# Decode attention on one core: halving the first half of K twice, and reading it from one PSUM bank

## Chip, cores, metric

One core of a Trainium2 chip. The metric is the device time of one execution in microseconds. "Ratio" below is the mean time of one kernel's runs over the mean of the other's runs of the same rounds, so it is not quite the ratio of the medians that I quote. Each comparison has its own runs of the kernel before, on the same chip.

## The reference

Attention with one query row per head: 8 x 32 = 256 heads, 4096 keys and values of 128 each, all bf16.

```python
B, H, Sq, Skv, Dh = 8, 32, 1, 4096, 128
def reference(q, k, v):
    scale = q.shape[-1] ** -0.5
    scores = jnp.einsum('bhqd,bhkd->bhqk', q, k) * scale
    attn = _softmax(scores, axis=-1)
    return jnp.einsum('bhqk,bhkd->bhqd', attn, v)
```

Every byte of K and V is used once. There is no reuse, so the kernel has to read 537 MB and do very little with each byte.

## The kernel before

A tile is eight heads: 16 partitions per head, 256 key rows on each partition (C = 256), 64 KB per partition. There are NT = 32 tiles of K and 32 of V, and SLOTS = 3 buffers that both share.

A K tile is worked on like this. VectorE multiplies it with the query in place, then adds the upper half of the 128 columns to the lower half (width 64), and for part of the tile once more (width 32). TensorE then adds what is left: it multiplies slices of 8 columns with an identity matrix and accumulates them in one bank of PSUM, the memory that matmuls write to (512 sums per partition and bank). VectorE reduces the bank's last axis to one score per key row.

```python
UC = 64; DS = 512 // UC; NU = C // UC          # 64 rows x 8 sums in a bank, 4 parts of a tile

def width_of(t, u):
    return D // 4 if u >= NU // 2 and 0 < t < NT - 3 else D // 2

def product(t, lo, hi):                        # VectorE
    ...
    nc.vector.tensor_tensor(out=part, in0=part, in1=qb[:].to_broadcast([P, hi - lo, D]), op=ALU.mult)
    nc.vector.tensor_tensor(out=part[:, :, 0 : D // 2], in0=part[:, :, 0 : D // 2],
                            in1=part[:, :, D // 2 : D], op=ALU.add)
    if width_of(t, lo // UC) < D // 2:
        nc.vector.tensor_tensor(out=part[:, :, 0 : D // 4], in0=part[:, :, 0 : D // 4],
                                in1=part[:, :, D // 4 : D // 2], op=ALU.add)

def sum_over_d(t, u):                          # TensorE, then scores_of on VectorE
    ps = ps_s.tile([P, UC, DS], F32, name="ps", tag="ps")
    n = width_of(t, u) // DS
    for s in range(n):
        nc.tensor.matmul(ps[:], lhsT=ident[:],
                         rhs=kt[:, u * UC : (u + 1) * UC, s * DS : (s + 1) * DS],
                         start=(s == 0), stop=(s == n - 1))
```

So in tiles 1 to 28 the first half of the rows goes to TensorE at width 64 (two banks of eight matmuls), the second at width 32 (two banks of four).

The order within a steady tile, shortened:

```python
product(t, 0, 2 * Q); sum_over_d(t, 0); sum_over_d(t, 1)      # Q = C // 4
product(t, 2 * Q, 3 * Q); sum_over_d(t, 2)
scores_of(t, 0); scores_of(t, 1)
product(t, 3 * Q, C); sum_over_d(t, 3); scores_of(t, 2)
values_loop(t - 1)                 # TensorE, 64 matmuls over the V tile before
load("k", t + 1); load("v", t)     # each is issued when a buffer comes free
scores_of(t, 3); weights_of(t)
```

With three buffers, V tile t goes where K tile t was, and is issued when TensorE has summed the last part of K tile t. The K tile after next goes where V tile t - 1 was, and is issued when the loop over it ends.

Of the kernel before, what the change touches and what calls it, by code (L numbers as in the profile page):

```python
# [8 lines left out]
ALU = mybir.AluOpType  # L9
AX = mybir.AxisListType  # L10
BF16 = mybir.dt.bfloat16
F32 = mybir.dt.float32
# [13 lines left out]
def kernel(  # L26
# [7 lines left out]
    nc = tc.nc  # L34
    B, H, Sq, D = q.shape
    S = k.shape[2]
    P = nc.NUM_PARTITIONS
# [3 lines left out]
    C = S // PH  # L41
    NT = NH // G
    scale = float(D) ** -0.5
    UC = 64
    DS = 512 // UC
    NU = C // UC
    CB = 4
    RG = R * G
    NQ = NT // R
# [18 lines left out]
    ps_s = ctx.enter_context(tc.tile_pool(name="ps_s", bufs=3, space=bass.MemoryType.PSUM))  # L68
# [7 lines left out]
    ident = consts.tile([P, P], BF16, name="ident")  # L76
    nc.gpsimd.memset(ident[:], 0.0)
    nc.gpsimd.affine_select(
        out=ident[:], in_=ident[:], pattern=[[-1, P]], compare_op=ALU.not_equal,
# [6 lines left out]
        out=heads[:], in_=heads[:], pattern=[[-1, G], [0, PH]], compare_op=ALU.not_equal,  # L86
# [6 lines left out]
        out=own[:], in_=own[:], pattern=[[-PH, G]], compare_op=ALU.is_ge,  # L93
# [3 lines left out]
        out=own[:], in_=own[:], pattern=[[PH, G]], compare_op=ALU.is_ge,  # L97
# [5 lines left out]
        out=same[:].rearrange("p (h x) -> p h x", x=PH),  # L103
        in_=own[:].rearrange("p (b h) -> p h b", h=TB // PH)
        .rearrange("p h (o b) -> p h o b", o=1)
        .to_broadcast([P, TB // PH, PH, P // TB]),
        axis=AX.X, op=ALU.max,
# [4 lines left out]
    for j in range(TG):  # L112
        part = pick[j * AG : (j + 1) * AG, :, :, :]
        nc.gpsimd.affine_select(
            out=part, in_=part, pattern=[[-1, CB], [CB * G, R], [-CB, RG]],
# [6 lines left out]
        out=mine[:], in_=mine[:], pattern=[[PH * G, R], [-PH, RG]], compare_op=ALU.is_ge,  # L122
# [3 lines left out]
        out=mine[:], in_=mine[:], pattern=[[-PH * G, R], [PH, RG]], compare_op=ALU.is_ge,  # L126
# [9 lines left out]
    def behind_loop(made):  # L136

        if loops:
            tc.add_manual_dep(
                made.ins, loops[-1].name,  # L140
                mybir.DependencyInfo(
                    mybir.DependencyClass.NoSync, mybir.DependencyReason.SCHED_ONLY
                ),
            )
# [8 lines left out]
    def load(kind, t):  # L153
        src = k_t if kind == "k" else v_t
        buf = kv_pool.tile([P, C, D], BF16, name=f"{kind}t", tag="kv")
        c0 = 0
        for n in cuts.get((kind, t), [C]):
            dma = nc.sync.dma_start(buf[:, c0 : c0 + n, :], src[t, :, c0 : c0 + n, :])  # L158
            behind_loop(dma)
            c0 += n  # L160
            if kind == "k" and t == 0 and c0 == n:
                nc.sync.dma_start(q_all[:], q_n)
        assert c0 == C
        loads[kind, t] = buf
# [3 lines left out]
    def q_prep(t):  # L168
        x, p0 = divmod(t * G, P)
        qh = ps_q.tile([G, D], F32, name="qh", tag="qp")  # L170
        nc.tensor.matmul(  # L171
            qh[:], lhsT=ident[:, p0 : p0 + G], rhs=q_all[:, x, :], start=True, stop=True
        )
        qg = q_pool.tile([G, D], BF16, name="qg", tag="qg")
        nc.scalar.activation(out=qg[:], in_=qh[:], func=ACT.Copy)  # L175
        qp = ps_q.tile([P, D], F32, name="qp", tag="qp")
        nc.tensor.matmul(qp[:], lhsT=heads[:].rearrange("g h x -> g (h x)"), rhs=qg[:], start=True, stop=True)  # L177
        qb = q_pool.tile([P, 1, D], BF16, name="qb", tag="qb")
        nc.scalar.activation(out=qb[:, 0, :], in_=qp[:], func=ACT.Copy)  # L179
        qbs[t] = qb  # L180

    def width_of(t, u):


        return D // 4 if u >= NU // 2 and 0 < t < NT - 3 else D // 2

    def product(t, lo, hi):
        kt = loads["k", t]
        qb = qbs[t]
        part = kt[:, lo:hi, :]  # L190
        nc.vector.tensor_tensor(  # L191
            out=part, in0=part, in1=qb[:].to_broadcast([P, hi - lo, D]), op=ALU.mult
        )
        nc.vector.tensor_tensor(  # L194
            out=part[:, :, 0 : D // 2], in0=part[:, :, 0 : D // 2],
            in1=part[:, :, D // 2 : D], op=ALU.add,
        )
        if width_of(t, lo // UC) < D // 2:
            nc.vector.tensor_tensor(  # L199
                out=part[:, :, 0 : D // 4], in0=part[:, :, 0 : D // 4],  # L200
                in1=part[:, :, D // 4 : D // 2], op=ALU.add,
            )

    sums = {}

    def sum_over_d(t, u):
        kt = loads["k", t]
        ps = ps_s.tile([P, UC, DS], F32, name="ps", tag="ps")
        n = width_of(t, u) // DS
        for s in range(n):  # L210
            nc.tensor.matmul(  # L211
                ps[:], lhsT=ident[:],
                rhs=kt[:, u * UC : (u + 1) * UC, s * DS : (s + 1) * DS],
                start=(s == 0), stop=(s == n - 1),
            )
        sums[t, u] = ps

    scs = {}

    def scores_of(t, u):  # L220
        if u == 0:
            scs[t] = sc_pool.tile([P, C], F32, name="sc", tag="sc")
        made = nc.vector.tensor_reduce(  # L223
            out=scs[t][:, u * UC : (u + 1) * UC], in_=sums.pop((t, u))[:], axis=AX.X, op=ALU.add
        )
        if u == NU - 1:
            behind_loop(made)

    ws = {}
# [102 lines left out]
    def norm_of(n):  # L332
        zp = ps_z.tile([RG, 1], F32, name="zp", tag="zp")
        esum = esums.pop(n)
        for r in range(R):
            nc.tensor.matmul(
                zp[:], lhsT=mine[:, r, :], rhs=esum[:, r : r + 1], start=(r == 0), stop=(r == R - 1)
            )
        zps[n] = zp

    def recip_of(n):
        rzs[n] = small.tile([RG, 1], F32, name="rz", tag="rz")
        nc.vector.reciprocal(out=rzs[n][:], in_=zps.pop(n)[:])
# [34 lines left out]
    def finish_of(n):  # L378
        s, u = divmod(n, OB)
        if u == 0:  # L380
            stages[s] = o_pool.tile([RG, OB, D], BF16, name="stage", tag="stage")
        made = nc.scalar.activation(  # L382
            out=stages[s][:, u, :], in_=ops.pop(n)[:], func=ACT.Copy, scale=rzs.pop(n)[:, 0:1]
        )
        behind_loop(made)
# [5 lines left out]
            lo = u if (last and u == OB - 1) else 0  # L391
            nc.scalar.dma_start(o_n[s, :, lo : u + 1, :], stages[s][:, lo : u + 1, :])

    Q = C // 4

    load("k", 0)
    E = mybir.EngineType
    with tc.manual_schedule(engines={E.PE, E.DVE, E.Activation, E.SP}):
        q_prep(0)
        q_prep(1)  # L400
        for t in range(NT):
            loop = 0 < t <= LT
            v_last = t >= NT - 2
            n = t // R - 1
            if not loop:
                if t + 1 < NT:
                    load("k", t + 1)
                load("v", t)
            product(t, 0, 2 * Q if loop else Q)
            if not loop:  # L410
                sum_over_d(t, 0)
            if 0 < t - 1 <= LT:
                if (t - 1) % R == 0:
                    norm_of(n)
                if t > 1:
                    result_of(t - 2)
            if t + 2 < NT:
                q_prep(t + 2)
            if loop:
                sum_over_d(t, 0)  # L420
            else:
                product(t, Q, 2 * Q)
            sum_over_d(t, 1)
            if not loop:
                scores_of(t, 0)
            product(t, 2 * Q, 3 * Q)
            sum_over_d(t, 2)
            if loop:
                scores_of(t, 0)
            scores_of(t, 1)  # L430
            if t > 2 and t % R == 1:
                recip_of(n)
            product(t, 3 * Q, C)
            sum_over_d(t, 3)
            scores_of(t, 2)
            if loop:
                values_loop(t - 1)
                load("k", t + 1)
                load("v", t)
            if v_last:  # L440
                values_of(t - 1, 0, C)
            scores_of(t, 3)
            weights_of(t)
            if t > 2 and t % R == 1:
                finish_of(n)
            if t > 0:
                copy_of(t - 1)
                if t > 2 and t % R == 1:
                    store_of(n)
                if not loop:  # L450
                    if t % R == 0:
                        norm_of(n)
                    result_of(t - 1)
        values_of(NT - 1, 0, C // 2)
        norm_of(NQ - 1)
        recip_of(NQ - 1)
        values_of(NT - 1, C // 2, C - LAST)
        copy_of(NT - 1)
        result_of(NT - 1)
        finish_of(NQ - 1)  # L460
        store_of(NQ - 1)
# [30 lines left out]
```

## Time and profile before

| | before |
|---|---|
| median, 6 runs | 1251.79 us (1251.49 to 1251.90) |
| read from HBM | 536.94 MB, 430 GB/s over the span |
| busy | VectorE 82%, TensorE 63%, ScalarE 13% |
| VectorE waits for K | 139.9 us, 28 times |
| steady tile | 38.7 us |

The prediction shows the lines and reads them. One of its terms is the lead of a V load: the start of the next tile's product, which starts as its K lands, minus the issue of the V load before it. It says how long the V load has stood in the queue when the K load ahead of it is done.

### The profile page before, as it was taken

How to read it: one execution, taken by the hardware profiler on the slowest of the kernel's cores; microseconds unless marked ns; L12 is line 12 of the kernel's file. 1: busy time of each engine (PE TensorE's matmuls, PEld its weight loads, DVE VectorE, ACT ScalarE, POOL GpSimd, SP SyncE). 2: the span in 40 equal slices, each digit the busy share in tenths (PEclk: the TensorE clock that was granted, in tenths of full speed). 3: DMA queues.
4: the chain of work that ended last, by engine and by line, in shares of the span. 5: the costliest groups of instructions: out<-in, count | busy, mean ns of one | idle time of the engine just before them, and what ended most of it. 6: DMA issues, size and time to landing. Idle time of an engine off the chain costs nothing. (4 is left out here: it accounts for less than half of the span.)

```text
span 1250.2 us, 10842 instructions
## 1 busy us (share of the span) xinstructions
PE 786.8 (63%) x3116; PEld 299.6 (24%) x3116; DVE 1021.9 (82%) x495; ACT 166.1 (13%) x433; POOL 4.5 (0%) x24
## 2 busy tenths in 40 slices
PE   3366567666576655766558665577655776556755
PEld 1122123222232222322223222222222222212222
DVE  7887987878977789777798777987779877798783
ACT  0111011111011110111101111011110111101111
POOL 1000000000000000000000000000000000000000
PEclk9987788777888778877788777887778878779867
DMA  9999999999999999999999999999999999999997
GB/s 405 436 436 435 434 436 432 436 430 428 426 437 436 429 435 434 434 435 436 436 434 432 424 437 437 432 430 428 436 437 434 430 433 434 430 435 421 427 446 329
DMA packets 11432, 537.33 MB, mean 430 GB/s; under 512 B 1808, under 2 KB 2064, under 8 KB 2320
## 3 DMA queue, kind: packets, MB, share of 16 engines
q1 hardware_dynamic: 11072, 536.94, 99.5%
q8 instruction: 15, 0.25, 0.1%
q10 hardware_dynamic: 336, 0.07, 0.0%
q14 instruction: 9, 0.07, 0.0%
HBM read 536.94 MB, written 0.07 MB: 430 GB/s over the span
## 5 line engine op out<-in xcount | busy, mean ns | idle before, releaser
L191 DVE TENSOR_TENSOR kt<-kt,qb 128x8192 bf16<-128x8192 bf16 (+1 forms) x99 | 560.9, 5665 | 146.6 <-DMA kt<-in_k_dram 139.9
L211 PE MATMUL ps<-kt,ident 128*128 128x512 bf16 x800 | 278.4, 511 | 389.9 <-DVE kt L199 299.7
L294 PE MATMUL av<-vt,w 128*32 x1740 | 425.5, 397 | 4.6
L194 DVE TENSOR_TENSOR kt<-kt 128x4096 bf16<-128x4096 bf16 (+1 forms) x99 | 288.8, 2917 | 3.4
L294 PEld LDWEIGHTS av<-vt,w 128*32 x1740 | 173.4, 100 | 262.4 <-issue 119.5
L211 PEld LDWEIGHTS <-ident 128*128 128x128 bf16 x800 | 95.7, 120 | 565.4 <-issue 527.9
L223 DVE TENSOR_REDUCE sc<-ps 128x64 f32<-128x512 f32 x128 | 85.3, 685 | 54.0 <-PE ps L211 54.0
L248 ACT ACTIVATE e<-sc,nmax 128x256 bf16<-128x256 f32 x32 | 16.3, 508 | 706.7 <-DVE nmax L242 706.7
L255 ACT ACTIVATE w<-e,mine 128x256 bf16<-128x256 bf16 x256 | 105.6, 495 | 1.1
L199 DVE TENSOR_TENSOR kt<-kt 128x2048 bf16<-128x2048 bf16 x56 | 68.6, 1225 | 1.9
L351 ACT ACTIVATE comb<-av 32x512 bf16<-32x512 f32 (+1 forms) x32 | 18.8, 586 | 329.0 <-PEq L284 321.4
L280 PE MATMUL av<-vt,w 128*32 128x512 bf16 x116 | 47.2, 499 | 14.6 <-issue 13.1
L371 PE MATMUL op<-comb,pick 32*16 32x128 bf16 (+1 forms) x128 | 12.1, 213 | 20.7 <-ACT comb L351 20.7
L280 PEld LDWEIGHTS av<-vt,w 128*32 128x32 bf16 x116 | 6.9, 100 | 55.2 <-issue 55.2
L177 PE MATMUL qp<-qg,heads 8*128 8x128 bf16 x32 | 7.0, 217 | 16.7 <-ACT qg L175 16.7
L371 PEld LDWEIGHTS <-pick 32*16 32x16 bf16 (+1 forms) x128 | 8.7, 83 | 27.7 <-issue 27.3
L322 PE MATMUL av<-vt,w 128*32 128x512 bf16 x188 | 13.7, 418 | 2.3 <-DMA vt<-in_v_dram 2.3
L235 DVE TENSOR_REDUCE pmax<-sc 128x1 f32<-128x256 f32 x32 | 13.4, 420 | 1.1
L175 ACT ACTIVATE qg<-qh 8x128 bf16<-8x128 f32 x32 | 8.5, 266 | 33.5 <-PE qh L171 33.5
L171 PE MATMUL qh<-q_all,ident 128*8 128x128 bf16 x32 | 7.2, 225 | 8.7 <-DMA q_all<-in_q_dram 8.3
L179 ACT ACTIVATE qb<-qp 128x128 bf16<-128x128 f32 x32 | 8.9, 278 | 9.7 <-PE qp L177 9.7
L237 DVE TENSOR_SCALAR spread<-same,pmax 128x32 f32<-128x32 f32 x32 | 7.7, 242 | 1.1
(31 smaller groups left out, 47.7 us busy)
## 6 DMA issues: line engine op xcount, KB each, us to landing
kt<-in_k_dram SPq DMA_DIRECT2D x4, 4096.0 KB, 24.3
kt<-in_k_dram SPq DMA_DIRECT2D x4, 2048.0 KB, 13.0
vt<-in_v_dram SPq DMA_DIRECT2D x1, 4096.0 KB, 33.9
vt<-in_v_dram SPq DMA_DIRECT2D x1, 2048.0 KB, 38.5
vt<-in_v_dram SPq DMA_DIRECT2D x1, 1024.0 KB, 40.5
vt<-in_v_dram SPq DMA_DIRECT2D x1, 512.0 KB, 41.3
vt<-in_v_dram SPq DMA_DIRECT2D x31, 25.8
kt<-in_k_dram SPq DMA_DIRECT2D x29, 28.3
```

What stands on the lines that cost most here:

```text
L191: nc.vector.tensor_tensor(out=part, in0=part, in1=qb[:].to_broadcast([P, hi - lo, D]), op=ALU.mult)
L194: nc.vector.tensor_tensor(out=part[:, :, 0 : D // 2], in0=part[:, :, 0 : D // 2], in1=part[:, :, D // 2 : D], op=ALU.add,)
L199: nc.vector.tensor_tensor(out=part[:, :, 0 : D // 4], in0=part[:, :, 0 : D // 4], in1=part[:, :, D // 4 : D // 2], op=ALU.add,)
L211: nc.tensor.matmul(ps[:], lhsT=ident[:], rhs=kt[:, u * UC : (u + 1) * UC, s * DS : (s + 1) * DS], start=(s == 0), stop=(s == n - 1),)
L223: made = nc.vector.tensor_reduce(out=scs[t][:, u * UC : (u + 1) * UC], in_=sums.pop((t, u))[:], axis=AX.X, op=ALU.add)
L248: nc.scalar.activation(out=e[:], in_=sc[:], func=ACT.Exp, bias=nmax[:, 0:1], scale=scale, accum_out=esums[t // R][:, t % R : t % R + 1],)
L255: nc.scalar.activation(out=w[:, :, g, :], in_=e_g, func=ACT.Copy, scale=mine[:, 0, g : g + 1])
L280: pe.matmul(av, lhsT=wf[:, i * nw : (i + 1) * nw], rhs=vf[:, i * nv : (i + 1) * nv], **how)
L294: pe.matmul(av, lhsT=wf[:, bass.ds(ow + i * nw, nw)], rhs=vf[:, bass.ds(ov + i * nv, nv)], start=False, stop=False,)
L322: nc.tensor.matmul(avs[t][j * AG : (j + 1) * AG, :], lhsT=w[:, i, :, :], rhs=vt[:, c0 : c0 + CB, :], start=(i < TG), stop=(j not in group[ ...
L351: nc.scalar.activation(out=comb[0:n, :, :], in_=av[0:n, :, :], func=ACT.Copy)
L371: nc.tensor.matmul(ops[n][:], lhsT=pick[0:e, m, r, :], rhs=comb[0:e, m, :], start=(r == 0 and m == 0), stop=(r == R - 1 and m == CB - 1 an ...
```

## The change

The first half of the tile's rows is to be treated like the second: halved twice on VectorE, so that TensorE has half the matmuls. At width 32 and with 128 rows, the half fits one PSUM bank with four partial sums per row: eight matmuls instead of sixteen, and one reduction instead of two.

```diff
-    def width_of(t, u):
-        return D // 4 if u >= NU // 2 and 0 < t < NT - 3 else D // 2
+    def width_of(t, lo):
+        return D // 4 if 0 < t < NT - 3 else D // 2
 ...
-    def sum_over_d(t, u):
+    def sum_over_d(t, lo, hi):
         kt = loads["k", t]
-        ps = ps_s.tile([P, UC, DS], F32, name="ps", tag="ps")
-        n = width_of(t, u) // DS
+        ps = ps_s.tile([P, BANK], F32, name="ps", tag="ps")      # BANK = 512
+        ds = BANK // (hi - lo)
+        n = width_of(t, lo) // ds
         for s in range(n):
             nc.tensor.matmul(
-                ps[:], lhsT=ident[:],
-                rhs=kt[:, u * UC : (u + 1) * UC, s * DS : (s + 1) * DS],
+                ps[:], lhsT=ident[:], rhs=kt[:, lo:hi, s * ds : (s + 1) * ds],
 ...
-    def scores_of(t, u):
+    def scores_of(t, lo, hi):
+        ps = sums.pop((t, lo))[:].rearrange("p (c s) -> p c s", c=hi - lo)
         made = nc.vector.tensor_reduce(
-            out=scs[t][:, u * UC : (u + 1) * UC], in_=sums.pop((t, u))[:], axis=AX.X, op=ALU.add
+            out=scs[t][:, lo:hi], in_=ps, axis=AX.X, op=ALU.add
         )
 ...
             if loop:
-                sum_over_d(t, 0)          # and sum_over_d(t, 1)
+                sum_over_d(t, 0, HALF)
 ...
             if loop:
-                scores_of(t, 0)           # and scores_of(t, 1)
+                scores_of(t, 0, HALF)
```

(Cut: the same calls by row ranges instead of part numbers, the halvings written as a loop, and the tiles outside the loop, whose work is unchanged.)

More of the change, by code (lines that the diff above doesn't have):

```diff
@@ L43 @@
     scale = float(D) ** -0.5
-    UC = 64
-    DS = 512 // UC
-    NU = C // UC
+    BANK = 512
     CB = 4
@@ L193, in product @@
         )
-        nc.vector.tensor_tensor(
-            out=part[:, :, 0 : D // 2], in0=part[:, :, 0 : D // 2],
-            in1=part[:, :, D // 2 : D], op=ALU.add,
-        )
-        if width_of(t, lo // UC) < D // 2:
+        n = D
+        while n > width_of(t, lo):
+            n //= 2
             nc.vector.tensor_tensor(
-                out=part[:, :, 0 : D // 4], in0=part[:, :, 0 : D // 4],
-                in1=part[:, :, D // 4 : D // 2], op=ALU.add,
+                out=part[:, :, 0:n], in0=part[:, :, 0:n], in1=part[:, :, n : 2 * n], op=ALU.add
             )
     sums = {}
-    def sum_over_d(t, u):
+    def sum_over_d(t, lo, hi):
         kt = loads["k", t]
-        ps = ps_s.tile([P, UC, DS], F32, name="ps", tag="ps")
-        n = width_of(t, u) // DS
+        ps = ps_s.tile([P, BANK], F32, name="ps", tag="ps")
+        ds = BANK // (hi - lo)
+        n = width_of(t, lo) // ds
         for s in range(n):
             nc.tensor.matmul(
-                ps[:], lhsT=ident[:],
-                rhs=kt[:, u * UC : (u + 1) * UC, s * DS : (s + 1) * DS],
+                ps[:], lhsT=ident[:], rhs=kt[:, lo:hi, s * ds : (s + 1) * ds],
                 start=(s == 0), stop=(s == n - 1),
             )
-        sums[t, u] = ps
+        sums[t, lo] = ps
     scs = {}
-    def scores_of(t, u):
-        if u == 0:
+    def scores_of(t, lo, hi):
+        if lo == 0:
             scs[t] = sc_pool.tile([P, C], F32, name="sc", tag="sc")
+        ps = sums.pop((t, lo))[:].rearrange("p (c s) -> p c s", c=hi - lo)
         made = nc.vector.tensor_reduce(
-            out=scs[t][:, u * UC : (u + 1) * UC], in_=sums.pop((t, u))[:], axis=AX.X, op=ALU.add
+            out=scs[t][:, lo:hi], in_=ps, axis=AX.X, op=ALU.add
         )
-        if u == NU - 1:
+        if hi == C:
             behind_loop(made)
@@ L392, in store_of @@
             nc.scalar.dma_start(o_n[s, :, lo : u + 1, :], stages[s][:, lo : u + 1, :])
-    Q = C // 4
+    Q, HALF = C // 4, C // 2
     load("k", 0)
@@ L408 @@
                 load("v", t)
-            product(t, 0, 2 * Q if loop else Q)
-            if not loop:
-                sum_over_d(t, 0)
+            if loop:
+                product(t, 0, HALF)
+            else:
+                product(t, 0, Q)
+                sum_over_d(t, 0, Q)
             if 0 < t - 1 <= LT:
@@ L419 @@
             if loop:
-                sum_over_d(t, 0)
+                sum_over_d(t, 0, HALF)
             else:
-                product(t, Q, 2 * Q)
-            sum_over_d(t, 1)
-            if not loop:
-                scores_of(t, 0)
-            product(t, 2 * Q, 3 * Q)
-            sum_over_d(t, 2)
+                product(t, Q, HALF)
+                sum_over_d(t, Q, HALF)
+                scores_of(t, 0, Q)
+            product(t, HALF, HALF + Q)
+            sum_over_d(t, HALF, HALF + Q)
             if loop:
-                scores_of(t, 0)
-            scores_of(t, 1)
+                scores_of(t, 0, HALF)
+            else:
+                scores_of(t, Q, HALF)
             if t > 2 and t % R == 1:
                 recip_of(n)
-            product(t, 3 * Q, C)
-            sum_over_d(t, 3)
-            scores_of(t, 2)
+            product(t, HALF + Q, C)
+            sum_over_d(t, HALF + Q, C)
+            scores_of(t, HALF, HALF + Q)
             if loop:
@@ L441 @@
                 values_of(t - 1, 0, C)
-            scores_of(t, 3)
+            scores_of(t, HALF + Q, C)
             weights_of(t)
```

## The prediction

> **What bounds the kernel now.** I first read the page: engine shares, the row of the DMA engines, the bytes moved.
>
> ```profile
> span 1250.2 us, 10842 instructions
> ...
> PE 786.8 (63%) x3116; PEld 299.6 (24%) x3116; DVE 1021.9 (82%) x495; ACT 166.1 (13%) x433; POOL 4.5 (0%) x24
> ...
> DMA  9999999999999999999999999999999999999997
> ...
> HBM read 536.94 MB, written 0.07 MB: 430 GB/s over the span
> ```
>
> No compute engine is full: VectorE, the busiest, is at 82%. The DMA row stands at 9 in 39 of 40 slices. K and V are each read once, 256 heads x 4096 rows x 128 x 2 bytes x 2 = 536.9 MB, which is all that is read; there is no traffic left to save, and the change touches none.
>
> A full share can still be an average, so next I read who waits for whom, on the engines and then on the queue that issues the loads.
>
> ```profile
> PE ps L211 <- DVE kt L199: 299.7, 56, 8.1
> DVE kt L191 <- DMA kt<-in_k_dram: 139.9, 28, 6.3
> ...
> PE ps L211 <- DVE kt L194: 90.0, 41, 8.6
> ...
> DVE sc L223 <- PE ps L211: 54.0, 33, 3.9
> ```
>
> The columns are total us, times, longest. VectorE waits for a K tile 28 times, once in each of tiles 2 to 29, mean 139.9 / 28 = 5.0 us. TensorE mostly waits for VectorE, and VectorE waits for TensorE only 54.0 us in all. So per tile the order is: transfer first, VectorE second, TensorE third.
>
> What decides is whether the transfers wait for anyone. There are three K/V buffers, so each load waits for one to come free. The timeline of one steady tile, without the rows that don't matter:
>
> ```profile
> 618.41 0.33 SPq L158 DMA_DIRECT2D vt<-in_v_dram  x1
> ...
> 624.96 8.69 DVE L191 TENSOR_TENSOR kt<-kt,qb 128x16384 bf16<-128x16384 bf16 x1 [4.88 <-DMA kt<-in_k_dram]
> ...
> 633.69 4.42 DVE L194 TENSOR_TENSOR kt<-kt 128x8192 bf16<-128x8192 bf16 x1
> ...
> 635.26 0.33 SPq L158 DMA_DIRECT2D kt<-in_k_dram  x1
> ...
> 638.03 4.42 DVE L191 TENSOR_TENSOR kt<-kt,qb 128x8192 bf16<-128x8192 bf16 x1
> 638.17 3.61 PE L211 MATMUL ps<-kt,ident 128*128 128x512 bf16 x16 [1.17 <-DVE kt L194]
> ...
> 642.49 2.29 DVE L194 TENSOR_TENSOR kt<-kt 128x4096 bf16<-128x4096 bf16 x1
> 644.81 1.23 DVE L199 TENSOR_TENSOR kt<-kt 128x2048 bf16<-128x2048 bf16 x1
> 645.96 1.28 DVE L223 TENSOR_REDUCE sc<-ps 128x64 f32<-128x512 f32 x2
> ...
> 647.15 4.42 DVE L191 TENSOR_TENSOR kt<-kt,qb 128x8192 bf16<-128x8192 bf16 x1
> ...
> 657.11 0.33 SPq L158 DMA_DIRECT2D vt<-in_v_dram  x1
> ...
> 663.67 8.69 DVE L191 TENSOR_TENSOR kt<-kt,qb 128x16384 bf16<-128x16384 bf16 x1 [4.89 <-DMA kt<-in_k_dram]
> ```
>
> The reader is to see three intervals here. The period is 663.67 - 624.96 = 38.71 us; one K and one V tile are 16.78 MB, so that is 433 GB/s with no gap. The V load that goes into the just-finished K tile's buffer is issued at 657.11, 6.56 us before the K load ahead of it in the queue lands (663.67). The next K load is issued when the loop over the previous V tile ends (635.26); V, issued at 618.41, lands by the median of its group 25.8 us later, at 644.2, so K is 8.9 us early. Both loads always join a queue that isn't empty: that lead is the quantity to follow. The smallest V lead that I found is the first one, 80.95 - 74.82 = 6.1 us.
>
> The kernel is bound by its DMA throughput; the head (the first product starts at 9.53) and the tail (last V chunk used at 1246.0) are outside the changed tiles.
>
> **What the Trainium skill says.** "DMA: Bandwidth & Descriptors", section "Where 436 GB/s comes from", gives 435 GB/s as the ceiling of the 16 ports into SBUF. The trace agrees: 433 GB/s in a steady tile, so nothing is to be gained beyond it. "VectorE: DVE Perf Modes", section "Side-by-side: where the cycles go for N=2048 bf16", gives 1224 ns for a two-operand bf16 instruction at two elements a cycle with about 150 fixed cycles; this trace has 1225 ns for 2048 elements (L199) and 2292 ns for 4096 (L194), the same slope, with runs of 32 as with runs of 64. "SBUF — State Buffer", section "Who interferes with whom", says that DMA doesn't contend with compute engines in SBUF. The trace doesn't contradict it: steady 40 us windows move 430 to 434 GB/s, and the window from 10 to 50 us, where VectorE was busiest (36.7 of 40 us), moved 445 GB/s.
>
> **The change part by part.** The shorter width now holds for the whole K tile in tiles 1 to 28 (before: only its second half). Tiles 0 and 29 to 31 keep width 64. In tiles 1 to 29 the first half is one PSUM tile of 128 rows x 4 sums instead of two of 64 x 8.
>
> - Added, VectorE: one halving of 128 rows to 32 columns, 4096 results, in 28 tiles. There is no such row yet, but the 4096-result halving of L194 takes 2.29 us; runs of 32 cost no more by L199. With the start gap before L199 in the timeline (0.03) I take 2.32 us.
> - Removed, VectorE: one of two reductions of a 512-sum bank, in 29 tiles, 0.685 us each. The remaining one reads 512 inputs and writes 128 results; its cost is in its inputs, so I leave it at 0.685. In the timeline the pair takes from 645.96 to 647.15 = 1.19 us until the next product, a lone one 0.60 (1213.55 to 1214.15), so the path is shorter by 0.59.
> - Net per changed tile: 2.32 - 0.59 = +1.73 us on VectorE. Busy: 1021.9 + 28 x 2.29 - 29 x 0.685 = 1021.9 + 64.1 - 19.9 = 1066 us, 85%; 495 + 28 - 29 = 494 instructions.
> - Removed, TensorE: 8 of 16 matmuls of the first half in 28 tiles, 224 in all, 3116 to 2892, of the group of 800 leaving 576. The sixteen take 3.6 us at 638.17 and 5.0 us in other tiles; half of that is about 2 us a tile, 56 us, leaving some 730 us busy. They start 2.3 us later, behind the new halving, but lie beside a product of 4.42 us and two halvings before anybody reads them: nothing on the path.
> - Moved: the end of the K tile's last matmul, and with it the V issue, the V loop and the next K issue, all later by 1.73 us after the K landing. V lead: 6.56 - 1.73 = 4.8 us (smallest 4.4). K lead: 8.9 - 1.7 = 7.2 us. VectorE's wait for K: 5.0 - 1.73 = 3.3 us, total 139.9 - 28 x 1.73 = 91 us.
>
> What is a lead worth? A new load needs some time before its bytes flow. The 4 KB store at the end took 1.5 us from issue to landing, so as an estimate a lead under 2 us would leave the engines idle. 4.4 is above that: no transfer starts later. VectorE's 48 us disappear in its own waits for K, TensorE's 56 us in its waits for VectorE. The delay doesn't add up from tile to tile, because each K landing, set by the queue, starts the count again.
>
> At the end tile 29 loses one reduction (0.6 us earlier), which only lengthens a lead; the last V chunks are issued from 1198.6 on behind queued loads, and what follows the landing is unchanged. Sum: 0 on the path, give or take some tenths: 1251.6 us.
>
> **The rivals.**
> 1. VectorE becomes the bound. If all of the added time lay on the path: 28 x 1.73 = 48 us, 1300 us (+3.9%). Against it: VectorE waited for K 28 times of 28, the shortest wait that I saw 4.45 us, over twice the addition.
> 2. The queue runs dry at the hand-over, since the lead shrinks and a load may need longer to start than I estimate, the 16 engines not finishing together. If 0.5 us were lost in each of 28 tiles: 14 us, 1266 us (+1.1%), still within 2%. For it: the lead is the one margin that the change spends. Against: 4.4 us are left.
> 3. TensorE's relief shows: 56 us off would be 1195 us (-4.5%). Against: TensorE waits for VectorE 390 us, and a matmul sooner done lets no load start sooner; the change makes the V issue later, not earlier.
> 4. The added SBUF traffic slows the transfers. 1% would be 12 us. Against: the windows above.
>
> **Range and chances.** I expect the same time. Executions spread by 0.3 us; on the low side nothing can give more than tenths, so 1250.0. On the high side a slight form of rival 2 or 4, 0.1 us a tile, gives 3 us: 1254.5. Faster by over 2% needs more bandwidth than the trace has anywhere in its steady part: 0.01. Slower by over 2% (25 us) needs 0.9 us lost in each of 28 tiles although 4.4 us of lead stand there: 0.015. Within 2%: 0.975.
>
> **What would show it.** The DMA row still full and 430 GB/s; K landings 38.7 us apart; VectorE's wait for K 28 times, about 91 us; halvings of 4096 results by 32 at 2.29 us; V issued about 4.8 us ahead of the next product's start; 2892 matmuls. I'd be wrong if the K wait went to zero (rival 1), or if the period grew while VectorE still waits (2, 4). A reduction of 128 groups of four that takes well over 0.685 us would be a mis-sized term, but up to 3 us of it would be hidden.

## The result

| | before | after |
|---|---|---|
| median, 6 runs each | 1251.79 us | 1253.92 us |
| lowest to highest | 1251.49 to 1251.90 | 1252.82 to 1255.22 |

The ratio is 1.0017 (95% interval 1.0005 to 1.003). That is the same time by a limit of 2%, and within the stated range. But it isn't nothing: every run of the changed kernel is slower than every run of the other, and the runs spread six times as far. Repeated beside the experiments it was 1254.87 us (1253.55 to 1258.6, 5 runs) against 1251.70, ratio 1.0031 (1.0018 to 1.0045).

The page of the changed kernel (1252.82 us, its fastest run), the same rows as in the prediction:

```profile
span 1251.1 us, 10425 instructions
...
PE 751.6 (60%) x2892; PEld 270.0 (22%) x2892; DVE 1068.7 (85%) x494; ACT 166.1 (13%) x433; POOL 4.4 (0%) x24
...
DMA  9999999999999999999999999999999999999997
...
HBM read 536.94 MB, written 0.07 MB: 429 GB/s over the span
```

The waits of the changed kernel (total us, times, longest):

```profile
PE ps L207 <- DVE kt L195: 426.6, 96, 10.9
...
DVE kt L189 <- DMA kt<-in_k_dram: 91.0, 28, 4.7
```

VectorE has 46.8 us more to do and waits 48.9 us less for K: the added work went into its own idle time. TensorE lost 224 matmuls and waits longer. The timeline of one steady tile of the changed kernel:

```profile
620.51 0.33 SPq L156 DMA_DIRECT2D vt<-in_v_dram  x1
...
625.31 8.69 DVE L189 TENSOR_TENSOR kt<-kt,qb 128x16384 bf16<-128x16384 bf16 x1 [3.12 <-DMA kt<-in_k_dram]
...
634.04 6.75 DVE L195 TENSOR_TENSOR kt<-kt 128x8192 bf16<-128x8192 bf16 x2
...
640.71 4.42 DVE L189 TENSOR_TENSOR kt<-kt,qb 128x8192 bf16<-128x8192 bf16 x1
640.84 1.91 PE L207 MATMUL ps<-kt,ident 128*128 128x512 bf16 x8 [1.90 <-DVE kt L195]
...
648.63 0.69 DVE L219 TENSOR_REDUCE sc<-ps 128x128 f32<-128x512 f32 x1
```

The two halvings (x2) now take 6.75 us where one took 4.42, eight matmuls follow them, and one reduction of 0.69 us stands where the pair stood. The lead is 625.31 - 620.51 = 4.80 us; before it was 6.56.

### The profile page after: what moved, and what is told of

Same layout as the page of the kernel before. It is cut to its first block, busy times and chain, and to the rows that moved or that the text cites. A ratio compares the mean times of both kernels' runs of the same rounds, so it can differ in the third digit from the quotient of the medians.

```text
span 1251.1 us, 10425 instructions
## 1 busy us (share of the span) xinstructions
PE 751.6 (60%) x2892; PEld 270.0 (22%) x2892; DVE 1068.7 (85%) x494; ACT 166.1 (13%) x433; POOL 4.4 (0%) x24
## 5 line engine op out<-in xcount | busy, mean ns | idle before, releaser
L207 PE MATMUL ps<-kt,ident 128*128 128x512 bf16 x576 | 243.4, 586 | 426.9 <-DVE kt L195 426.6
L195 DVE TENSOR_TENSOR kt<-kt 128x4096 bf16<-128x4096 bf16 (+1 forms) x183 | 421.6, 2304 | 6.2
L207 PEld LDWEIGHTS <-ident 128*128 128x128 bf16 x576 | 65.5, 128 | 597.6 <-DVE kt L195 489.8
L219 DVE TENSOR_REDUCE sc<-ps 128x64 f32<-128x512 f32 (+1 forms) x99 | 68.0, 686 | 55.3 <-PE ps L207 55.3
```

The costliest lines, as they stand in the source:

```text
L195: nc.vector.tensor_tensor(out=part[:, :, 0:n], in0=part[:, :, 0:n], in1=part[:, :, n : 2 * n], op=ALU.add)
L207: nc.tensor.matmul(ps[:], lhsT=ident[:], rhs=kt[:, lo:hi, s * ds : (s + 1) * ds], start=(s == 0), stop=(s == n - 1),)
L219: made = nc.vector.tensor_reduce(out=scs[t][:, lo:hi], in_=ps, axis=AX.X, op=ALU.add)
```

## The experiments

Twelve kernels ran, in three groups, each group on its own chip. Theories: **A**, the transfers bound the kernel and the change only spends lead; the 2 us come from leads that are too short. **B**, the 2 us are chance. **C**, VectorE's added traffic in SBUF, the memory that holds the tiles, slows the transfers a little.

### Is the added work really hidden? The same change where the transfers don't bind

Only half of each V tile is loaded and used in tiles 0 to 28, in the kernel before and in the changed one. Their outputs are wrong, which doesn't matter for the times.

```diff
-        for n in cuts.get((kind, t), [C]):
+        for n in [C // 2] if kind == "v" and t < LT else cuts.get((kind, t), [C]):
 ...
-        vf = loads["v", t][:].rearrange("p c d -> p (c d)")
+        vf = loads["v", t][:, 0 : C // 2, :].rearrange("p c d -> p (c d)")
 ...   # the loop over V: 2 + 4 x 7 + 2 matmuls instead of 2 + 10 x 6 + 2
```

> A wrong result on purpose: of V tiles 0 to 28 only the first half is loaded and used (the loop over V runs half as long). The transfers of a K and half a V tile take 12.58 MB / 433 GB/s = 29.0 us, less than VectorE's 33.8 us a tile, so VectorE should be the bound: about 1251.5 - 28 x 4.9 = 1115 us, nearly no wait for K. If something else bounds the kernel at 38.7 us a tile, it stays near 1251 us.

> The same cut of V in the changed kernel, wrong on purpose as well. If the change's cost is hidden only because the transfers bound the kernel, it must show here in full: 28 x 1.73 = 48 us over half_v_before, about 1163 us. If the added halving is free for another reason (VectorE's work overlapping, the removed TensorE work paying for it), the two come out within 10 us of each other.

Measured: 1105.66 us (1105.38 to 1105.86, 4 runs) and 1153.99 us (1153.78 to 1154.13, 4 runs), against 1252.07 for the kernel before in full. Both are 9 us below the number expected, but the change costs 48.3 us here where 48 were expected. The timeline of two successive first products of VectorE, of the cut kernel before and then of the cut changed kernel; in neither kernel does VectorE wait for K at all:

```profile
515.21 8.66 DVE L192 TENSOR_TENSOR kt<-kt,qb 128x16384 bf16<-128x16384 bf16 x1
...
548.97 8.67 DVE L192 TENSOR_TENSOR kt<-kt,qb 128x16384 bf16<-128x16384 bf16 x1
```

```profile
504.14 8.67 DVE L190 TENSOR_TENSOR kt<-kt,qb 128x16384 bf16<-128x16384 bf16 x1
...
539.61 8.67 DVE L190 TENSOR_TENSOR kt<-kt,qb 128x16384 bf16<-128x16384 bf16 x1
```

The periods of these two are 33.76 and 35.47 us; over all 28 they are 33.73 and 35.49 us on average, 1.76 us more per tile. So the added work costs its full time where VectorE is the bound, and at full traffic some 46 of these 48 us are hidden behind the transfers.

### Each part alone

The bank alone: the first half stays at width 64, in one bank of 128 x 4, by sixteen matmuls.

```diff
-        return D // 4 if 0 < t < NT - 3 else D // 2
+        return D // 4 if lo >= C // 2 and 0 < t < NT - 3 else D // 2
```

> One part alone: the first half of K stays at width 64, but its 128 rows go into one PSUM bank with four sums each, by sixteen matmuls, read by one reduction. VectorE loses 0.6 us a tile, so the V lead grows from 6.5 to about 7.1 us and the mean wait for K from 5.0 to 5.6 us. Theories A, B and C: 1251 to 1252 us, the time of the kernel before, runs within 0.5 us. If VectorE were the bound it would be 17 us faster.

Measured: 1251.59 us (1251.44 to 1252.02, 5 runs), ratio 1.0 (0.9986 to 1.0013). The wait for K grew as expected and the time did not move; the saved reduction is worth nothing here either:

```profile
DVE kt L189 <- DMA kt<-in_k_dram: 155.6, 28, 6.9
```

The halving alone: the kernel before with width 32 in both halves, the first still in two banks read by two reductions.

```diff
-        return D // 4 if u >= NU // 2 and 0 < t < NT - 3 else D // 2
+        return D // 4 if 0 < t < NT - 3 else D // 2
```

> The other part alone: the first half halved twice, but still in two banks of 64 x 8 sums, here by four matmuls each, read by two reductions. VectorE 2.3 us more a tile than before, 0.6 us more than the changed kernel; V lead about 4.2 us, wait for K 2.6 us. Theory A: worse than the changed kernel, since the loss grows as the lead falls from 4.8 to 2.5 us: 1255 to 1264 us. Theory C: the same added traffic as the changed kernel, so the same time within 1 us, 1253 to 1256 us.

Measured: 1261.38 us (1257.85 to 1266.02, 5 runs), ratio 1.0067 (1.0054 to 1.0081). It has the changed kernel's halving and 0.6 us less lead, and costs 9.6 us over the kernel before where the whole change costs 2 to 3. Theory C expected no difference between them. VectorE still waited for K in all 28 tiles, so it wasn't full:

```profile
DVE kt L191 <- DMA kt<-in_k_dram: 87.3, 28, 4.5
```

### More VectorE work: where is the cliff?

One or two further halvings, into columns that nobody reads, so the result stays right.

```diff
+        if 0 < t < NT - 3 and lo == 0:
+            for _ in range(1):                      # dose2: range(2)
+                nc.vector.tensor_tensor(
+                    out=part[:, :, 64:96], in0=part[:, :, 64:96], in1=part[:, :, 96:128], op=ALU.add
+                )
```

> The changed kernel with one more halving of 4096 results in tiles 1 to 28, into columns that nobody reads (result still right): VectorE 2.33 us more a tile. The wait for K should fall to 0.8 us a tile (22 us in all), the V lead to 2.5 us. Theory A: some us more than the changed kernel, 1255 to 1262. Theory B: 1251.5 to 1254. Theory C: about twice the 2 us, 1256. If VectorE were already the bound: 65 us more, 1318.

> The changed kernel again, as the anchor of this group. Theory A (the transfers bound the kernel; the change only shortens the lead with which the V load joins the queue, 6.5 to 4.8 us, and the shorter lead costs a little): 1253 to 1255 us, runs spread by over 1 us. Theory B (the 2 us were chance of one chip): within 0.5 us of the kernel before. Theory C (more VectorE traffic in SBUF slows the transfers by about 0.1%): 1253 to 1255 us too.

Measured: after_again is quoted above (1254.87). dose1 took 1279.75 us (1276.42 to 1284.48, 5 runs), ratio 1.0228 (1.0207 to 1.0249): far more than theory A in the form of "some us" or theory C allowed, and far less than a full VectorE. The wait for K did not fall to 22 us:

```profile
DVE kt L189 <- DMA kt<-in_k_dram: 56.3, 28, 4.8
```

VectorE is idle and the transfers are late at once. The timeline of dose1, one tile, shows how. The V load was issued 2.63 us before the next product started, and the K tile after that came 40.66 us later instead of 38.7:

```profile
636.79 0.33 SPq L156 DMA_DIRECT2D vt<-in_v_dram  x1
...
639.42 8.69 DVE L189 TENSOR_TENSOR kt<-kt,qb 128x16384 bf16<-128x16384 bf16 x1 [0.95 <-DMA kt<-in_k_dram]
...
680.08 8.69 DVE L189 TENSOR_TENSOR kt<-kt,qb 128x16384 bf16<-128x16384 bf16 x1 [2.90 <-DMA kt<-in_k_dram]
```

After such a slip VectorE waits longer, the next V load has a longer lead, and that tile often loses nothing.

> The changed kernel with two more halvings of 4096 results in tiles 1 to 28, unread: VectorE 4.65 us more a tile than the changed kernel, 1.5 us more than the 3.1 us that it still waits for K. VectorE becomes the bound: 28 x 1.5 = 42 us over the changed kernel, about 1296 us, waits for K near zero. If the margin were not those 3.1 us: at most 1262 us when it is larger, over 1330 us when it is smaller.

Measured: 1302.71 us (1301.32 to 1304.05, 4 runs), 7 us above the 1296 expected. VectorE waits for K 13.5 us in all and the tiles come 40.5 us apart (median): VectorE is nearly the bound.

From the traces of the kernels that load in the same way, tile by tile (27 intervals between K landings each; the profiled run's time is given because runs spread):

| profiled run | usual lead, us | intervals over 39.2 us | K 29 lands at | time of that run |
|---|---|---|---|---|
| bank_only | 7.1 | 2 | 1129.9 | 1251.55 |
| before | 6.6 | 3 | 1130.1 | 1251.86 |
| the changed kernel, first group | 4.8 | 4 | 1130.4 | 1252.82 |
| after_again | 4.8 | 6 | 1133.3 | 1254.87 |
| halve_only | 4.1 to 4.6, where nothing slipped just before | 12 | 1142.6 | 1266.02 |
| dose1 | 2.2 to 3, likewise | 16 | 1157.3 | 1279.75 |

K 29 is the last K tile whose start is timed in this way. after_again lost 3.2 us up to it and 3.0 us in all: its whole loss lies in these hand-overs, the changes from one load to the next. The first profile of the changed kernel, of its fastest run, had lost only 0.3 of its 1.0 us by then, so a single trace at this lead shows little; the dose is what shows it. In halve_only the 14 intervals after a lead of 4.0 to 4.6 us have a mean of 39.7 us, the 6 after 4.6 to 5.2 us 38.9; in dose1 the 12 after less than 3 us have 40.5, the 4 after more than 5.2 us 38.7.

The change shortens the lead of the K loads too (8.9 to 7.4 us), so the landings of single loads were looked at. A K or V tile that loses nothing lands 19.35 us after the load ahead of it. Added up, the V tiles of dose1 took 25.9 us more than that and its K tiles 6.1 (kernel before: 2.7 and 1.5): most of the loss is in the V loads, those with the short lead.

### Giving the lead back

This is the test of theory A: the same VectorE work, but V is loaded in two halves, the first issued as soon as the first half of the K tile in its buffer is summed. For that the three buffers become fixed tiles, so that waits follow the part that is overwritten.

```diff
+    slots = [kv_pool.tile([P, C, D], BF16, name=f"kv{i}") for i in range(SLOTS)]     # bufs=1
 ...
-        buf = kv_pool.tile([P, C, D], BF16, name=f"{kind}t", tag="kv")
+        buf = slots[len(loads) % SLOTS]
-        for n in cuts.get((kind, t), [C]):
+        for n in cuts.get((kind, t), [C // 2] * 2 if kind == "v" else [C]):
```

> The changed kernel with its lead given back: the three K/V buffers are fixed tiles, and each V load is issued as two halves, the first as soon as the first half of the K tile in that buffer is summed. Same VectorE work. Theory A: back to 1251 to 1252 us or a little less, runs within 0.5 us; the first V half is issued some 20 us before the K load ahead of it lands. Theory C: stays at 1253 to 1255 us. Theory B: no difference from any.

> The kernel before with the V load issued in two halves, the first one when the first half of the K tile in its buffer is summed. Theory A: a lead longer than 6.5 us brings at most a little, 1250 to 1251.5 us. Theories B and C: as the kernel before, 1251.5 to 1252 us. If twice as many V transfers cost something at each start, over 1253 us.

Both came out wrong (relative error 0.17) and slow, 1302.66 and 1302.40 us, and prove nothing about the theories. With fixed buffers the order of the program decides what a load overwrites, and outside the loop V 30 is loaded ahead of the work on K 30, in K 30's place. Besides the wrong result this made one wait of 55 us:

```profile
DVE kv L190 <- DMA kv<-in_v_dram: 55.1, 1, 55.1
```

Mended, that one load follows its tile's sums:

```diff
-                load("v", t)
+                if t != NT - 2:
+                    load("v", t)
 ...
+            if t == NT - 2:
+                load("v", t)
             if v_last:
```

> split_after mended: there V 30 was loaded over K 30 before it was read (the fixed buffers made that order mine to keep), which gave the wrong result and one wait of 55 us at the end; now that one load comes after the sums of its tile. The changed kernel's VectorE work, with V loads issued as two halves, the first some 20 us ahead. Theory A (a V load that joins the queue less than about 5 us before the transfer ahead of it lands loses transfer time): 1250 to 1252 us, runs within 0.6 us. Theory C (VectorE's added traffic slows transfers): 1253 to 1256 us, as the changed kernel. If two halves cost time at each start: over 1256 us.

> split_before mended in the same way: the kernel before with early half loads of V. Theory A: its lead of 6.5 us was already enough, so 1250 to 1252 us, at most 0.1% faster than before. If the lead of 6.5 us still cost something in the tiles where a transfer is late: 1246 to 1250 us.

> dose1 (one more unread halving a tile, 28 us slower than the kernel before) with the same early half loads of V. VectorE needs about 38.0 us a tile, the transfers 38.7. Theory A: nearly all of the 28 us come back, 1250 to 1256 us, with VectorE waiting about 0.8 us a tile for K. Theory C, or a VectorE that is simply full: stays at 1275 to 1285 us.

In split_after_b, the changed kernel so mended, the first half joins the queue 21.26 us before the next product starts. The second comes no earlier than the whole load did, but now stands behind the first half:

```profile
604.55 16.81 SPq L157 DMA_DIRECT2D kv<-in_v_dram  x2
...
625.81 8.69 DVE L190 TENSOR_TENSOR kv<-kv,qb 128x16384 bf16<-128x16384 bf16 x1 [3.10 <-DMA kv<-in_k_dram]
```

| kernel | whole V loads | V in two early halves |
|---|---|---|
| before | 1251.77 us (same rounds) | 1253.74 us (1253.68 to 1253.79, 5 runs) |
| changed | 1254.87 us, spread 5.0 us | 1253.79 us (1253.66 to 1254.05, 5 runs) |
| changed + one more halving (dose1) | 1279.75 us, spread 8.1 us | 1254.82 us (1254.49 to 1255.10, 5 runs) |

(The right-hand column and its kernel before are of one group; the other two of the left-hand column are of another, beside a kernel before of 1251.70.)

My number for split_after_b and split_before_b missed: I expected 1250 to 1252, and the split form itself costs 2 us. split_before_b shows it without any change to VectorE's work. The two halves of a V tile take 19.42 us from landing to landing (median) where a whole one takes 19.35, and 0.07 us in each of 31 tiles make the 2 us. The packets of a half are of 32 KB instead of 64: two take 2 x 1.218 us, one of 64 KB takes 2.420 (medians).

What theory A said is nevertheless plain in the differences within the right-hand column. With the first half some 20 us ahead the change costs 0.05 us instead of 2 to 3, its spread falls from 5.0 to 0.4 us, and dose1 gets 25 of its 28 us back with the same VectorE work. There VectorE waits for K 1.1 us a tile (0.8 was expected):

```profile
DVE kv L190 <- DMA kv<-in_k_dram: 31.2, 28, 2.4
```

Theory C falls: the same added traffic in SBUF costs 0.05 us here, and dose1's further 4096 results a tile 1.03 us. Theory B falls with the two intervals that exclude 1 and the order of halve_only, the changed kernel and before. The K loads of split_dose1 are a check from the other side: 22 of them had a lead of only 4.6 to 6 us over the V half ahead, and lost nothing. One thing is left untested: the split form changes the size of V's packets along with the time of issue, and halves that are issued late were not run.

What happens at a hand-over can be read in part from the packets in the traces, which have a start, a duration and a size, but not their engine. The 16 engines don't end a load together: in the kernel before, the ends of one K load lie 2.3 us apart (median; 4.2 at most). Where engines stood idle at the issue, the first packet of the V load started 0.96 us after it (dose1 and dose2). So at the short leads of dose1 the queue does run dry: each engine stands idle 0.5 us on average at a hand-over to V, 13.8 us over 27 of them. The rest is slower packets. Of the 64 KB packets between 60 and 1100 us, 25 of 6867 took over 2.6 us in the kernel before, 115 in after_again, 282 in halve_only and 372 in dose1, 353 of these within 9 us after a V issue. In after_again an engine stands idle only 1.0 us over all 27 hand-overs: at a lead of 4.8 us the queue doesn't run dry, its first packets are slow. Why they are stays open.

No version beat the kernel before; bank_only equals it.

## Why the prediction was right, and which step was mis-sized

- **What binds.** Right: the transfers. With half of V taken away the same change costs 48.3 us; 28 x 1.73 = 48 had been worked out.
- **VectorE's terms.** Right. Halving of 4096 results by runs of 32: 2292 ns (2.29 said). One reduction of 128 groups of four: 684 ns (685 said). Busy 1068.7 us (1066 said), 494 instructions, 1.76 us more a tile where VectorE is the bound (1.73 said).
- **Where it goes.** Right: the wait for K is 91.0 us over 28 waits (91 said), the lead 4.80 us (4.8 said), the K landings a median of 38.71 us apart.
- **TensorE.** The direction was right, the size not: 751.6 us busy, 730 said. The first halves alone gave what was said: in 28 tiles sixteen matmuls of 5.04 us on average became eight of 3.13, 53 us (56 said). But the 56 groups of four in the second halves, which the change doesn't touch, went from 1.59 to 1.89 us, 16 us in all, at a granted clock of 0.50 in them against 0.65. It lies off the path, as predicted.
- **What a lead is worth.** This step was mis-sized. From the 4 KB store's 1.5 us I estimated that a lead under 2 us would leave the engines idle and that 4.4 us stood clear above it. The runs show losses from about 5 us down: at 4.8 a few tiles slip (four and six of 27 intervals over 39.2 us in the two profiles, three in the kernel before), at 4.0 to 4.6 the interval after is 39.7 us on average, below 3 us 40.5. What the estimate left out is in the packets: the engines end a load at different times, 2.3 us apart, and the first packets after a short lead are slow. The issue-to-landing time of a small, lone store said nothing about how far ahead an 8 MB load has to be queued.
- **The rivals.** Rival 2, a loss at the hand-over, is the one that took place, at 2 to 3 us in all rather than 14; that the queue itself runs dry is seen only at shorter leads (halve_only and dose1, 3.9 and 13.8 us per engine over 27 hand-overs). Rival 1 was not near: VectorE still waited 3.1 us in a usual tile, 2.67 at least. Rival 3 failed: TensorE's relief bought nothing. Rival 4 is theory C. One figure held against it was misread: 445 GB/s from 10 to 50 us is no rate, since the view counts packets by their start and their share there comes to 1.03 of the engines; the two whole tiles that were loading then took 19.36 and 19.34 us, as elsewhere.

The time, 1253.92, is 2.3 us over the 1251.6 predicted and inside the range because the range had been opened upwards for a slight form of rival 2 or 4. The middle of the forecast rested on the estimate of the lead, which was wrong; the 0.1 us a tile that the range allowed for it was a guess, and that it sufficed is partly luck.

## What to carry to other kernels

When transfers bind, work moved between engines is free only as long as the loads that it delays still join the queue early enough: read the lead of each load over the landing of the one before it, and treat it as the margin, not the idle time of the engine. Here VectorE had 5 us idle a tile, but only about 1.7 of them could be spent at little cost; one more halving cost 25 us though VectorE would still have had idle time. A wider spread of the runs (5 us where it had been 0.7) was the first sign that the margin was used up.

## What the Trainium skill lacked or had wrong

- "DMA: Bandwidth & Descriptors", section "Anatomy of one DMA — SWDGE (gpsimd) path", puts a fixed cost of about 2 us on a DMA that GpSimd issues. No page says how far ahead the next large load must be issued to keep the transfers going. Here, with 8 MB loads issued from SyncE's queue, a lead of 6.6 us lost no more than one of 7.1, 4.8 us lost 2 to 3 us over 28 tiles, 2.2 to 3 us lost 28 us. Nor does a page say how far apart the 16 engines end one load: 2.3 us here (median), at most 4.2.
- The same page, section "Bandwidth", measures single transfers by size. Cutting each 8 MB V load into two of 4 MB, both queued well ahead, cost 2.0 us over 31 tiles (1253.74 against 1251.77); it has no figure for large loads queued one behind the other.
- "VectorE: DVE Perf Modes", section "The perf-mode tier table (the rule you actually need)", gives `tensor_reduce` one rate and doesn't say what the grouping does. Here 64 groups of eight and 128 groups of four from one bank took 685 and 684 ns.
- "SBUF — State Buffer", section "Who interferes with whom", was borne out: with the lead given back, the change's added traffic cost 0.05 us in 1254.
